# A Strassen-like feed-forward kernel: one of the seven products divided once more, over unit pairs and both passes

## The chip, the cores and the metric

The kernel runs on one core of a Trainium2 chip. The metric is the device time of one execution in microseconds, the median of several runs. The core's engines work side by side, each in its own program order: TensorE (PE, matmuls into eight PSUM banks of 128 x 512 f32), VectorE (DVE), ScalarE (ACT), GpSimd (POOL) and SyncE (SP, which issues the DMAs). They wait for each other through semaphores.

## What is computed

A gated feed-forward block on 2048 tokens, with Dm = 1024 and Df = 3584:

```python
def reference(x, w_gate, w_up, w_down):
    g = jnp.einsum("bsd,df->bsf", x, w_gate)
    u = jnp.einsum("bsd,df->bsf", x, w_up)
    h = _gelu(g) * u
    return jnp.einsum("bsf,fd->bsd", h, w_down)
```

All inputs are bf16, the output too.

## The kernel before

**Seven products for eight.** The gate and up products are done by the Strassen-Winograd scheme: two matrices cut into 2 x 2 blocks are multiplied with seven block products in place of eight, at the price of sums of blocks. The two raw products (of blocks as they are) run in bf16, the others in f32r, a full-rate form of f32, since sums of bf16 values don't fit bf16.

**Tiling.** The 2048 tokens go in two passes (`NPASS`) of 1024, two column halves of 512 each. The 3584 features go in 14 units (`NU`) of 256, two row halves of 128 each; the contraction over 1024 is halved too (`KH` = 4 blocks of 128 each). In a unit, every product is done for gate and up, with four matmuls of 512 columns each:

- two raw products (`raw_products`, L190), done for two units at once, at the end of every odd unit: 32 bf16 matmuls,
- p6 = s2·t2, p5 = s1·t1, p7 = s3·t3, p3 = s4·tb and p4 = A22·T4 (`unit`, L208): eight f32r matmuls each.

The t are sums of blocks of x, made by DVE once for each pass (`sums_t`; t4 is the last of a chain t1, t2, t4). The s are sums of blocks of the weights, eight POOL operations for each unit, one unit ahead (`make_s`, called in `prepare`, L658, right behind p5). `sa` is the block A22, cast to f32r by ACT.

**From banks to hT.** Products that belong together are added inside a bank where that is possible. Otherwise ACT copies a bank to SBUF (`snap`, L108; tiles p1, u2, p5), and DVE adds the copy to another bank (`add`; tiles sum). Then ACT makes the gelu of the gate half (`gelu`, L180), and DVE multiplies it with the up half into hT (`times`). Banks come in four pairs, which change their roles from unit to unit (L635). A product can begin only when the bank's last reader is done.

**Order.** The order on PE, DVE, POOL and SP is that of the program, by `manual_schedule`; ACT's too in the units. In pass 0, units 2 and up also make the sums of w_down that the second half of a pass needs (`keep_part`, L266): ACT copies a block into a bank that is free for a moment, DVE subtracts (tiles m, three for each unit). They stand behind p6 and ahead of p5's snaps and of `prepare`. They are kept in HBM (td). Small tiles in SBUF come from one ring of 52 slots (`slot`, L83): a new tile waits for the readers of the one that had the slot.

**Second half of a pass.** `down` (L464) multiplies hT with w_down, by a scheme of its own, and writes the output. In `more`, which it calls, x of the next pass is transposed by DMA and the sums t and s of the next pass's first unit are made.

**Helpers.** Every DVE sum goes through `dve` (L91), every POOL sum through `pool` (L94), every matmul through `matmul` (L112), so that the profile's rows are told apart by tiles.

Of the kernel before, what the change touches and what calls it, by code (L numbers as in the profile page):

```python
# [10 lines left out]
def kernel(  # L11
# [23 lines left out]
    nc = tc.nc  # L35
# [21 lines left out]
    NPASS = S // (2 * N)  # L57
    NU = NFB // 2
    NWARM = 7
    H, Q, R2 = NJ // 2, N // 2, range(2)  # L60
    SLOTS = 52
    LAG = 3
# [20 lines left out]
    def slot(shape, dtype, name):  # L83
        return kpool.tile(shape, dtype, name=name, tag="k")
# [5 lines left out]
    def dve(out, a, b, op):  # L90
        nc.vector.tensor_tensor(out=out, in0=a, in1=b, op=op)  # L91
# [9 lines left out]
    def cast(src, name, shape=None):  # L101
        t = slot(shape or [P, N], f32r, name)
        nc.scalar.copy(out=t, in_=src)  # L103
        return t

    def snap(ps, name):
        t = slot([P, N], f32, name)
        nc.scalar.copy(out=t, in_=ps)  # L108
        return t
# [40 lines left out]
    def sums_s(w, eng):  # L150
        GU = range(2)
        sh = [P, KH, P]
        a11, a21 = [[w[:, i, :KH, h : h + P] for i in GU] for h in (0, P)]
        a12, a22 = [[w[:, i, KH:, h : h + P] for i in GU] for h in (0, P)]
        return Sums(
            how={
                "s1": lambda q, GU=GU: [new(eng, a21[i], a22[i], ADD, "s1", sh) for i in GU],
                "s2": lambda q: [new(eng, q["s1"][i], a11[i], SUB, "s2", sh) for i in GU],
                "s3": lambda q: [new(eng, a11[i], a21[i], SUB, "s3", sh) for i in GU],
                "s4": lambda q: [new(eng, a12[i], q["s2"][i], SUB, "s4", sh) for i in GU],  # L160
                "sa": lambda q: [cast(a22[i], "sa", sh) for i in GU],
            }
        )

# [5 lines left out]
        t.make("t1", "t2", "t3", "tb", "t4")  # L170
        return t

    def make_s(w, eng):
        s = sums_s(w, eng)
        s.make("s1", "s2", "s3", "sa", "s4")
        return s

    def gelu(src):
        g = slot([P, N], f32, "g")
        nc.scalar.activation(g, src, ACT.Gelu_apprx_tanh)  # L180
        return g

    def times(fb, c, g, u):
        dve(hT[:, fb // NJ, fb % NJ, c, :], g, u, MUL)

    def product(ps, lhs, rhs, start):
        for k in range(KH):
            matmul(ps, lhs[:, k, :], rhs[k], start and k == 0, k == KH - 1)

    def raw_products(e, c, xT, w):  # L190
        for i in range(2):
            product(e[i], w[:, i, :KH, :P], [xT[0][:, k, :] for k in range(KH)], True)
        p1 = [snap(e[i], "p1") for i in range(2)]
        for i in range(2):
            b21 = [xT[0][:, KH + k, :] for k in range(KH)]
            product(c[i], w[:, i, KH:, :P], b21, True)
        return p1

    def add(ps, other):
# [4 lines left out]
    def finish_raw(u, c, p1):  # L204
        g, up = add(c, p1)
        times(2 * u, 0, gelu(g), up)

    def unit(u, banks, s, t, late, after_p5, aside, keep, ahead_of_p4, behind_p4):  # L208
        GU = range(2)
        e, c, d = banks  # L210
        aside(-2)
        g, up = late() if late else (None, None)
        aside(-1)
        for i in GU:
            product(e[i], s["s2"][i], t["t2"], False)
        aside(0)
        keep(0, c[0])
        u2 = [snap(e[i], "u2") for i in GU]
        if late:
            g = gelu(g)  # L220
        c11 = g, up
        keep(1, c[0])
        keep(2, c[1])
        c = d
        for i in GU:
            product(c[i], s["s1"][i], t["t1"], True)
        p5 = [snap(c[i], "p5") for i in GU]
        after_p5()
        for i in GU:
            product(e[i], s["s3"][i], t["t3"], False)  # L230
        g, up = new(dve, e[0], p5[0], ADD, "sum", dtype=f32), banks[1][not late]
        dve(up, e[1], p5[1], ADD)
        if late:
            times(2 * u, 0, *c11)
        for i in GU:
            product(c[i], s["s4"][i], t["tb"], False)
        times(2 * u + 1, 1, gelu(g), up)
        aside(1)
        g, up = add(c, u2)
        times(2 * u, 1, gelu(g), up)  # L240
        ahead_of_p4()
        for i in GU:
            product(e[i], s["sa"][i], t["t4"], False)
        behind_p4()
        times(2 * u + 1, 0, gelu(e[0]), e[1])

    td = dpool.tile([P, NJ, 3, N], f32, name="td")  # L250
    wraw, made = {}, {}

    def fetch_wd(js):
        big = None
        for j in js:
            if j < NJ - 2:
                wraw[j] = [slot([P, Dm], bf16, "raw") for _ in range(2)]
            else:
                if big is None:
                    big = wpool.tile([P, 4, Dm], bf16, name="w")  # L260
                n = 2 * (j - NJ + 2)
                wraw[j] = [big[:, n + kh] for kh in range(2)]
            for kh in range(2):
                nc.sync.dma_start(out=wraw[j][kh], in_=wdn[:, kh, j, :])
# [367 lines left out]
            return []  # L632
        return list(range(u - 2, NJ if u == NU - 1 else u - 1))

    E, K, C, F = odd, cc, dd, even  # L635

    def loaded(u):
        if u not in ws:
            ws[u] = load_w(u)
        return ws[u]  # L640

    def raw_of(u, e):
        p1 = raw_products(e, K, xT, loaded(u))
        return lambda: finish_raw(u, K, p1)

    for ip in range(NPASS):
        with tc.manual_schedule(engines={ENG.Activation}):
            if ip == 0:
                ws = {1: w, 2: ahead}
                late = lambda: add(cc, nxt["p1"])  # L650
            else:
                raw_of(0, F)()
                raw_of(1, C)()
            for u in range(1 if ip == 0 else 0, NU):
                js = making(u) if ip == 0 else []
                first = (ip, u) == (0, 1)

                def prepare():  # L658
                    if first:
                        pool_behind(t["t4"][-1])  # L660
                    if u + 1 < NU:
                        nxt["s"] = make_s(loaded(u + 1), pool)
                    if len(js) == 1:
                        store_made(js[0])
                    for j in js[1:]:
                        keep_whole(j)
                    if ip == 0:
                        fetch_wd(making(u + 1))

                def keep(part, ps):  # L670
                    if js:
                        keep_part(js[0], part, ps)

                def aside(part):
                    if first and part < 0:
                        rest_of_0(part + 2)
                    if part == 0 and u + 2 < NU:
                        loaded(u + 2)
                    if part == 0 and "t4" not in t:
                        t.make("t4")  # L680

                def ahead_of_p4():
                    if u % 2 and u + 1 < NU:
                        raw_of(u + 1, F)()
                        nxt["c11"] = raw_of(u + 2, C)

                def behind_p4():
                    if "c11" in nxt:
                        nxt.pop("c11")()

                if u % 2 and not first:
                    E, K, C = C, E, K
                banks = (E, K, C) if u % 2 else (F, K, E)
                unit(
                    u, banks, s, t, late if first else None, prepare, aside, keep,
                    ahead_of_p4, behind_p4,
                )
                s = nxt.pop("s", None)

        last = ip == NPASS - 1  # L700
        got, nxt = {}, {}

        def more(step):
            if last:
                return
            if step in (-1, 0, 2):
                store_made({-1: NJ - 3, 0: NJ - 2, 2: NJ - 1}[step])
            if step == 0:
                xT[:] = new_x()
            if step >= 24 and step % 2 == 0 and step // 2 - 12 < len(moves):  # L710
                c, ko = moves[step // 2 - 12]
                transposing(xT, c, ko, (2 * (ip + 1) + c) * N)
            if step == 50:
                ws.clear()
                ws.update({n: load_w(n) for n in range(2)})
            if step == 58:
                got["s"] = make_s(ws[0], dve)
            if step == 62:
                got["t"] = make_t(xT)

        down(ip, F + K, C + E, last, more)
        E, K, C, F = K, E, F, C
        if not last:
            t, s = got["t"], got["s"]

# [28 lines left out]
```

## Time and profile before

| | |
|---|---|
| median of 3 runs | 539.14 us (538.97 to 539.33) |
| the profiled execution | 539.29 us |
| its span | 537.5 us |
| mean granted clock of TensorE | 0.999 |
| PE busy | 532.7 us (99%), 2451 matmuls |
| DVE busy | 356.3 us (66%) |
| ACT busy | 258.1 us (48%) |
| POOL busy | 259.3 us (48%) |
| DMA | 93.30 MB, mean 174 GB/s |

The profile is of one execution. The span runs from the first to the last recorded instruction; 1.8 us lie outside of it. Of each engine it gives busy time and share of the span. The chain that ended last is followed back from the last instruction to what released it. In the rows of operations, "out<-in" names the tiles, then the shapes; xN is the number of instructions in the row, and where a row of the timeline ends in brackets, the engine was idle that long before it, and the name behind the arrow is what ended the idle time.

Two facts of order that are used below: unit 2 begins at 40.65 us, unit 3 at 49.72, unit 4 at 65.73, unit 5 at 74.80; the raw products of units 4 and 5 run from 56.98 to 63.71.

### The profile page before, as it was taken

The numbers are of one execution on the slowest core, as the hardware profiler recorded it, in microseconds if no ns is written. First come the engines' busy times: TensorE is split into PE (matmuls) and PEld (weight loads), VectorE is DVE, ScalarE is ACT, GpSimd is POOL, SyncE is SP. The second block draws the span as 40 slices with busy tenths as digits, with TensorE's granted clock in tenths as the row PEclk, the third lists the DMA queues.
The fourth block names the chain that finished last, engine by engine and source line by source line (L and its number), as shares of the span: only waits on it lengthen the run. The fifth ranks groups of instructions, "written<-read, shape, count | busy, mean of one in ns | idle before, by whom it ended". The sixth has DMA issues, their size and how long they took to land.

```text
span 537.5 us, 7573 instructions
## 1 busy us (share of the span) xinstructions
PE 532.7 (99%) x2451; PEld 382.4 (71%) x2451; DVE 356.3 (66%) x536; ACT 258.1 (48%) x457; POOL 259.3 (48%) x243
## 2 busy tenths in 40 slices
PE   8999999999999999999999999999999999999997
PEld 4568686867777746888868677776868685478887
DVE  2986766767676894595855464555554639979844
ACT  2556675666666410265355555555555551113340
POOL 1179966677773500000087767676766600000194
PEclk9999999999999999999999999999999999999999
DMA  9675666759482999999873233242520049573752
GB/s 245 156 186 168 186 177 176 218 136 262 131 234 71 383 357 298 308 197 275 264 187 88 78 80 81 77 119 50 145 57 23 2 130 390 204 236 88 243 169 70
DMA packets 108199, 93.30 MB, mean 174 GB/s; under 512 B 17280, under 2 KB 93056, under 8 KB 108160
## 3 DMA queue, kind: packets, MB, share of 16 engines
q1 hardware_dynamic: 108160, 92.82, 59.6%
q8 instruction: 20, 0.33, 0.3%
q14 instruction: 19, 0.16, 0.1%
HBM read 74.45 MB, written 15.20 MB: 167 GB/s over the span
## 4 chain that ended last, share of the span: by engine, by line
PE 98%; DMA 1%; SPq 0%; DVE 0%; issue 0%
PE bank L112 98%; DMA xn<-in_x_dram 1%; SPq L538 0%; DVE st L91 0%; PE bank L545 0%
## 5 line engine op out<-in xcount | busy, mean ns | idle before, releaser
L94 POOL TENSOR_TENSOR s<-w 128x512 fp32r<-128x512 bf16 x102 | 119.0, 1188 | 163.0 <-PE bank L112 113.5
L112 PE MATMUL bank<-t,s 128*128 128x512 f32 x648 | 151.7, 390 | 0.0
L112 PEld LDWEIGHTS bank<-t,s 128*128 128x128 f32 x648 | 121.7, 188 | 25.4
L112 PE MATMUL bank<-xT,w 128*128 128x512 bf16 (+1 forms) x504 | 109.7, 376 | 0.0
L108 ACT COPY p<-bank 128x512 f32<-128x512 f32 x124 | 69.8, 590 | 45.2 <-PE bank L112 45.1
L91 DVE TENSOR_TENSOR sum<-bank,p 128x512 f32<-128x512 f32 x54 | 37.3, 691 | 79.4 <-PE bank L112 78.3
L112 PEld LDWEIGHTS <-w 128*128 128x128 bf16 x504 | 48.1, 98 | 58.1 <-issue 3.4
L91 DVE TENSOR_TENSOR hT<-g,bank 128x512 bf16<-128x512 f32 x112 | 76.8, 688 | 17.6 <-PE bank L112 4.5
L180 ACT ACTIVATE g<-sum 128x512 f32<-128x512 f32 x81 | 51.4, 635 | 74.5 <-DVE sum L91 74.2
L94 POOL TENSOR_TENSOR q<-q 128x256 fp32r<-128x256 f32 x28 | 21.1, 788 | 80.0 <-PE bank L112 79.4
L112 PE MATMUL bank<-q 128*128 128x512 f32 x240 | 59.0, 389 | 0.0
L94 POOL TENSOR_TENSOR s<-w,s 128x512 fp32r<-128x512 bf16 x50 | 57.7, 1175 | 0.0
L94 POOL TENSOR_TENSOR s<-s,w 128x512 fp32r<-128x512 f32 x50 | 57.2, 1166 | 0.0
L112 PE MATMUL bank<-t,sa 128*128 128x512 f32 x216 | 55.9, 401 | 0.0
L112 PE MATMUL bank<-tb,s 128*128 128x512 f32 x216 | 53.3, 389 | 0.0
L108 ACT COPY u<-bank 128x512 f32<-128x512 f32 x62 | 35.5, 589 | 34.3 <-PE bank L112 34.2
L112 PEld LDWEIGHTS bank<-q 128*128 128x128 f32 x240 | 45.1, 188 | 9.3
L112 PE MATMUL bank<-raw,hT 128*128 128x512 bf16 x224 | 48.7, 379 | 0.0
L112 PEld LDWEIGHTS bank<-t,sa 128*128 128x128 f32 x216 | 40.6, 188 | 9.4
L103 ACT CAST tb<-raw 128x512 fp32r<-128x512 bf16 x28 | 17.2, 624 | 62.6 <-DMA raw<-in_w_down_dram 34.1
L112 PEld LDWEIGHTS bank<-tb,s 128*128 128x128 f32 x216 | 40.6, 188 | 8.4
L91 DVE TENSOR_TENSOR bank<-bank,p 128x512 f32<-128x512 f32 x54 | 37.7, 699 | 8.8 <-PE bank L112 6.2
(60 smaller groups left out, 493.8 us busy)
## 6 DMA issues: line engine op xcount, KB each, us to landing
raw<-in_w_down_dram SPq DMA_DIRECT2D x76, 256.0 KB, 5.1
q<-td SPq DMA_DIRECT2D x60, 256.0 KB, 4.9
w<-in_w_gate_dram SPq DMA_DIRECT2D x27, 512.0 KB, 5.9
w<-in_w_up_dram SPq DMA_DIRECT2D x27, 512.0 KB, 7.0
td<-m SPq DMA_DIRECT2D x12, 768.0 KB, 4.6
w<-td SPq DMA_DIRECT2D x6, 1024.0 KB, 10.1
out_dram<-st SPq DMA_DIRECT2D x32, 128.0 KB, 1.7
td<-w SPq DMA_DIRECT2D x2, 768.0 KB, 6.3
```

What stands on the lines that cost most here:

```text
L91: nc.vector.tensor_tensor(out=out, in0=a, in1=b, op=op)
L94: nc.gpsimd.tensor_tensor(out=out, in0=a, in1=b, op=op)
L103: nc.scalar.copy(out=t, in_=src)
L108: nc.scalar.copy(out=t, in_=ps)
L112: nc.tensor.matmul(ps, lhsT=lhs, rhs=rhs, start=start, stop=stop, skip_group_check=True)
L180: nc.scalar.activation(g, src, ACT.Gelu_apprx_tanh)
```

## The change

For the units 4 to 11, the product p4 is divided once more. Two neighbouring units a and b (4/5, 6/7, 8/9, 10/11: `SPLIT`) give two row blocks, the two passes give two column blocks, the contraction of four k blocks is halved: a 2 x 2 x 2 product of its own, for which seven half products are done in place of eight. A half product has four matmuls (two k blocks, gate and up).

- **Pass 0** does five of the seven at the end of unit b (`split_first`): A11·B11, A12·B21, s2·i2, sh·i4, s3·i3. That is 20 matmuls where p4 of the two units had 16. Two sums (z2, z3) that the other pass needs are copied by ACT and stored in HBM (dz).
- **Pass 1** does the other two in unit b, between p5 and p7 (`split_second`): s1·i1 and s4·t4[2:], 8 matmuls for 16. The stored sums are loaded during unit a, and DVE adds the product to all four.
- **Sums of weights** for a pair (`split_sums`): three more POOL operations for each pair and pass, behind `make_s` of unit b. In pass 1 the cast `sa` of these units goes; in pass 0 that of unit b becomes a half one (`sh`).
- **Sums over the passes.** The columns of B come from t4 of both passes, so t4 of pass 1 is made in pass 0. x of pass 1 is transposed by 16 DMAs in units 1 to 3 (`next_x`), into the part of hT that is still unused. In `prepare` of units 2, 3 and 4, DVE makes t4 of pass 1 from it (`next_t4`, three operations for each of four k blocks: 3, 6, 3). In `prepare` of units 4 and 5, DVE makes the inner sums i1 to i4 (`inner_i`, four operations each). i1 is stored in HBM (di) and loaded in pass 1 (`load_i1`).
- **Banks.** The four pairs get other names and another rotation. In pass 0 the raw products behind a divided pair run in another order: the first raw product of both units, then the second of each. Some hT products read other banks than before.

The core of the diff:

```diff
+    SPLIT = (4, 6, 8, 10)
+    NEXT_X = {1: (0,), 2: (1, 2), 3: (3,)}
+    NEXT_T4 = {2: ((0,), ()), 3: ((1, 2), ()), 4: ((3,), (0,)), 5: ((), (1,))}
...
+    def split_sums(wa, wb, ip):
+        ka, kb = slice(KH, KH + 2), slice(KH + 2, NKB)
+        a11, a12, a21, a22 = [w[:, :, k, P:] for w in (wa, wb) for k in (ka, kb)]
+        sh = [P, 2, 2, P]
+        q = {"s1": new(pool, a21, a22, ADD, "s1", sh)}
+        q["s2"] = new(pool, q["s1"], a11, SUB, "s2", sh)
+        if ip == 0:
+            q["s3"] = new(pool, a11, a21, SUB, "s3", sh)
+        else:
+            q["s4"] = new(pool, a12, q["s2"], SUB, "s4", sh)
+        return q
...
-    def unit(u, banks, s, t, late, after_p5, aside, keep, ahead_of_p4, behind_p4):
+    def unit(u, banks, s, t, late, after_p5, aside, keep, mid, behind_p7, p4):
...
         after_p5()
+        mid()
         for i in GU:
             product(e[i], s["s3"][i], t["t3"], False)
         g, up = new(dve, e[0], p5[0], ADD, "sum", dtype=f32), banks[1][not late]
         dve(up, e[1], p5[1], ADD)
+        more = behind_p7()
...
+    def split_first(a, ea, eb, z, s, sp, t):
+        sa = s["a"]["sa"]
+        half(z, lambda i, k: sa[i][:, k], t["t4"][:2], True)
+        z1 = [snap(z[i], "z1") for i in range(2)]
+        half(ea, lambda i, k: sa[i][:, 2 + k], t["t4"][2:], False)
+        g, up = plus(ea, z1)
+        half(z, lambda i, k: sp["s2"][:, i, k], t["i2"], False)
+        z2 = [snap(z[i], "z2") for i in range(2)]
+        gl = gelu(g)
+        times(2 * a + 1, 0, gl, up)
+        half(eb, lambda i, k: s["b"]["sh"][:, i, k], t["i4"], False)
+        half(z, lambda i, k: sp["s3"][:, i, k], t["i3"], False)
+        z3 = [snap(z[i], "z3") for i in range(2)]
+        g, up = plus(eb, z3)
+        for n, zs in enumerate((z2, z3)):
+            for i in range(2):
+                nc.sync.dma_start(out=dz[:, a // 2, n, i], in_=zs[i])
+        times(2 * a + 3, 0, gelu(g), up)
...
+    def split_second(a, ea, y, sp, t, z):
+        half(y, lambda i, k: sp["s1"][:, i, k], t["i1"], True)
+        half(ea, lambda i, k: sp["s4"][:, i, k], t["t4"][2:], False)
+        for n in range(2):
+            for i in range(2):
+                dve(z[n][i], y[i], z[n][i], ADD)
+        g, up = plus(ea, z[0])
+        times(2 * a + 1, 0, gelu(g), up)
...
+    def next_t4(k):
+        lo, hi = [[hT[:, 1, 6 + kk, c, :] for c in range(2)] for kk in (k, KH + k)]
+        q = new(dve, lo[1], lo[0], SUB, "t1")
+        q = new(dve, hi[1], q, SUB, "t2")
+        later[k] = new(dve, hi[0], q, SUB, "t4")
+
+    def inner_i(t, k):
...
+        b11, b21 = t["t4"][k], t["t4"][2 + k]
+        b12, b22 = later[k], later[2 + k]
+        i1 = new(dve, b12, b11, SUB, "i1")
+        dve(t["i2"][k], b22, i1, SUB)
+        nc.sync.dma_start(out=di[:, k], in_=i1.bitcast(f32))
+        dve(t["i3"][k], b22, b12, SUB)
+        t["i4"].append(new(dve, b21, t["i2"][k], SUB, "i4"))
...
                     if ip == 0:
                         fetch_wd(making(u + 1))
+                        if u in NEXT_T4:
+                            for k in NEXT_T4[u][0]:
+                                next_t4(k)
+                            for k in NEXT_T4[u][1]:
+                                inner_i(t, k)
```

## The prediction

> **What bounds the kernel now.** I read the page first: busy times, then the chain that ended last.
>
> ```profile
> span 537.5 us, 7573 instructions
> PE 532.7 (99%) x2451; PEld 382.4 (71%) x2451; DVE 356.3 (66%) x536; ACT 258.1 (48%) x457; POOL 259.3 (48%) x243
> ...
> PE 98%; DMA 1%; SPq 0%; DVE 0%; issue 0%
> ```
>
> TensorE (PE) carries 98% of the chain. The view of PE's waits holds only two, 0.8 and 0.6 us, both at the start. So a matmul taken out is worth its whole time, and any wait that the change brings to PE is added whole: there is no idle time on PE to take it up. The question is whether the other engines still finish ahead of PE. Next, the timeline of PE in units 5 and 6:
>
> ```profile
> 74.80 5.60 PE L112 MATMUL bank<-t,s 128*128 128x512 f32 x24
> 80.24 1.97 PE L112 MATMUL bank<-tb,s 128*128 128x512 f32 x8
> 82.06 7.08 PE L112 MATMUL bank<-xT,w 128*128 128x512 bf16 x32
> ```
>
> From start to start, 24 f32r matmuls take 5.44 us, 0.2267 each, and 32 bf16 ones 6.73. Then the windows view, with one row for each pair of units (25.1 us of PE work), says how much room the helpers have:
>
> ```profile
> 40.65:65.70 25.05, 25.05 (x113) 18.08 (x112) 17.35 (x26) 16.13 (x31) 25.05 (x24) 1.00 0.65 190
> 65.70:90.80 25.10, 25.10 (x113) 18.08 (x112) 17.45 (x26) 16.29 (x31) 18.57 (x17) 1.00 0.66 189
> 300.00:325.00 25.00, 25.00 (x114) 18.01 (x112) 13.41 (x21) 13.85 (x25) 18.01 (x17) 1.00 0.32 85
> ```
>
> The columns are PE, PEld, DVE, ACT, POOL. VectorE (DVE) has 7.7 us free in a pair of pass 0 and 11.6 in one of pass 1; GpSimd (POOL) has none in units 2 and 3, some 6.5 us later. Last, the timeline of DVE in unit 3, where the change puts most:
>
> ```profile
> 53.61 1.49 DVE L91 TENSOR_TENSOR m<-bank,m 128x512 fp32r<-128x512 f32 x2 [0.80 <-ACT bank L272]
> 55.01 0.68 DVE L91 TENSOR_TENSOR sum<-bank,p 128x512 f32<-128x512 f32 x1
> 55.61 0.69 DVE L91 TENSOR_TENSOR bank<-bank,p 128x512 f32<-128x512 f32 x1
> 56.70 0.69 DVE L91 TENSOR_TENSOR hT<-g,bank 128x512 bf16<-128x512 f32 x1 [0.40 <-ACT g L180]
> ```
>
> A DVE operation lasts 0.69 us; one that doesn't need the result just before it starts 0.60 us after it, one that does 0.80 (m, two in 1.49). The queue is in program order. In that order prepare stands behind the m's and ahead of the sum that takes p7 out of its bank, so what the change adds in prepare delays that sum.
>
> **What the change removes: matmuls.** The order of instructions of the two programs shows 2451 PE matmuls before and 2435 after. For each of the four pairs, pass 0 does 20 half-product matmuls in place of 16, pass 1 does 8 in place of 16: +16 and -32 in all. 16 x 0.2267 = **-3.6 us**. These sit in pairs 4 to 11, whose f32r matmuls have one rate.
>
> **What it adds beside PE.** DVE gets 68 operations: 20 in pass 0's units 2 to 5 (3, 6, 7, 4: next_t4 and inner_i), 16 in pass 0's pairs, 32 in pass 1's. POOL gets 24 (split_sums, 3 for each pair and pass, 1.13 each). ACT gets four. SP gets 16 transposes and 35 plain DMAs. I go by place.
>
> - Transposes of the next x, units 1 to 3: issued on SP, which idles between loads there; before's transposes take 1.1 to 1.3 us each to issue and land after 4.3. They land some microseconds before next_t4 reads them. 0; behind them on SP stand the raw loads of unit 3 (the one ending ACT's wait at 51.49), which at worst come 2 us late. I take 0.
> - Units 2 and 3, DVE alone. Unit 2: the m's end at 45.32; three dependent operations (2.2 us) put the p7 sum at 47.6, its end at 48.1 (PE lag included) where p4 would start at 47.91: +0.3. Unit 3: six operations (4.4 us) end at 59.5; then come the sum, the bank sum, the gelu on ACT and the hT product, which ends at 61.5. That product reads the bank that the next raw product of unit 4 writes, which PE reaches at 59.8: +1.8. Two further banks of the raws, handed on by DVE the same way, +0.37 each. Together **+2.8**.
> - Units 4 and 5, DVE alone: seven operations (4.9 us) and four (2.9), in a pair that has 7.7 us free in all and also takes 4 extra sums. Same order of reasoning, bank by bank: p5 of unit 5 waits for unit 4's hT product +1.6; p7 of unit 5 for the snaps of u2, which on ACT stand behind two late gelus, +1.4; p3 +0.3; the first half product of split_first for the hT product of unit 5, +3.0; the snap of z +0.5. **+6.8**. As a check: 15 x 0.7 = 10.5 us of added DVE work against 7.7 of room leaves 2.8 even if nothing was in the wrong order, and order costs the rest, as the m's come late in a unit (their ACT copies need the bank that PE frees).
> - Pairs 6 to 11 in pass 0: the snap of z1 (0.59) ahead of the half product that reuses z, about 0.15 each: **+0.45**.
> - Pass 1: DVE has 13.4 us in a pair, gains 8 x 0.69 and p4's banks need more hops: about 19 to 21 of 23.3 (25.1 less eight matmuls). The hT product ahead of the second raw bank is late by 0.15 to 0.4: **+1.6** for four pairs. POOL goes to 19 operations, 21.5 of 23.3 us: still covered, with 1.8 us to spare.
> - Stores and loads of z and i1 (256 KB, 4.6 to 5 us from issue to landing here) are issued half a unit or more ahead: 0; uncovered, 5 us once.
>
> **DVE against POOL.** The 20 operations in units 2 to 5 read two tiles in SBUF; nearly all of before's DVE operations there read a PSUM bank instead, and are not slowed by POOL (0.69 all through 30 to 66 us with POOL busy). Where two-SBUF operations met POOL, the timeline shows:
>
> ```profile
> 270.04 2.50 DVE L91 TENSOR_TENSOR t<-xT,t 128x512 fp32r<-128x512 bf16 x4
> 270.35 4.30 POOL L94 TENSOR_TENSOR s<-w 128x512 fp32r<-128x512 bf16 x2 [86.06 <-PE bank L112]
> ...
> 507.50 1.22 DVE L91 TENSOR_TENSOR q<-hT,q 128x512 fp32r<-128x512 bf16 x1
> 508.65 1.22 DVE L91 TENSOR_TENSOR q<-hT 128x512 fp32r<-128x512 bf16 x1
> ```
>
> At 270 DVE kept going and POOL's two operations took 4.30 us for the usual 2.27; at 507, where POOL ran two of half the size, DVE took 1.22 for 0.69. So one waits for the other, and both outcomes exist. next_t4 is a chain (t1, t2, t4), which leaves DVE empty for 0.1 us between operations, so I expect POOL to get in. A first operation then waits half a POOL operation (0.55), each dependent one up to 1.13 + 0.6 - 0.8 = 0.95 more. Unit 2, POOL back to back: 0.55 + 2 x 0.95 = 2.4. Unit 3, where POOL has about two operations of s(4) left: 1.5. Unit 4: 1.5; unit 5: 0.6. **+6.0**; bounds 0 (as at 270) and +12 (every one of the 20 meets POOL, and PE pays two thirds).
>
> The Trainium skill (SBUF — State Buffer, "Who interferes with whom") says that such a DVE operation and a GpSimd operation that reads SBUF block each other fully, and that the one that starts first goes first; by that rule alone, POOL being busy, the sum would take the +6.0. The rows at 507 agree, the row at 270 only if the four count as one.
>
> **Sum.** 539.3 (the profiled execution; its span is 537.5, the median of the runs 539.14) - 3.6 + 2.8 + 6.8 + 6.0 + 0.45 + 1.6 = **553.4 us**.
>
> **Rivals.**
> - *DVE keeps the memory to itself* (as at 270): term 6.0 falls to about 1. 548.4. For it: same shapes as at 270. Against: the chain's gaps.
> - *Faster: the bursts are covered.* DVE and ACT work off the delay before PE comes to the bank, because PE's next products need other banks first. Then only unit 2's 0.3, 0.45 and about 1 in pass 1 are left: 537.4. For it: 7.7 us free per pair, and POOL and DMA nowhere late. It decides if unit 3's hT product ends before 59.8, that is if its six operations take under 2.7 us in place of 4.4; for that they would have to start before the m's end. Against: program order.
> - *Every operation meets POOL*: +12 in place of +6.0, 559.4, with PE pauses of several microseconds. The page's row of granted clock is full speed throughout, with no pause over 0.8 us. The Trainium skill (TensorE: Matmul & The Clock Gate, Part 1) puts the return to half speed after an idle window of about 3.4 us; nothing in this trace tests it, and by it each such pause would cost about 1.7 us more.
> - *POOL is late in pass 1*: at a mean of 1.30 us per operation (DVE's two-SBUF sums beside it) 19 take 24.7 of 23.3 us: +1.4 a pair, 5.6 in all: 557.4 (553.4 - 1.6 + 5.6).
> - *It doesn't do what it says*: the count of matmuls excludes this.
>
> **Chances.** Forecast (550 to 557) 0.42; DVE keeps (544 to 550) 0.27; every operation meets POOL 0.10; POOL late in pass 1 0.06; covered 0.12; within 0.2% of before (about what a measurement of this kernel can tell from no change), the two sides cancelling, 0.03. Slower 0.85, faster 0.12. The range leaves out the covered and equal cases and the worst of the upper: 542 to 561; the forecast alone has 550 to 557.
>
> **What would show it.** Right: PE waits of 10 us or more in all between 45 and 100 us, released by DVE hT products and sums; PE busy 3.6 us lower; added DVE operations at over 1 us where POOL works; next to nothing in pairs 6 to 11 of pass 0. Wrong: PE without waits at 60 and at 85 us (covered), added operations at 0.69 (DVE keeps), or PE waiting in pass 1 for s tiles (POOL late).

## The result, and the profile after

The changed kernel takes 563.13 us (median of 4 runs, 562.28 to 564.38) against 539.24 for the one before: a ratio of 1.0446, with a 95% interval of 1.0422 to 1.0469. That is 23.9 us slower, where 14.2 were forecast; it lies 2.1 us above the range. The profiled execution took 564.38, its span is 562.5.

The page of the changed kernel, the same three lines as before:

```profile
span 562.5 us, 7718 instructions
PE 538.2 (96%) x2414; PEld 380.5 (68%) x2435; DVE 403.2 (72%) x604; ACT 258.1 (46%) x461; POOL 290.5 (52%) x267
...
PE 74%; DVE 7%; DMA 7%; ACT 6%; issue 3%; POOL 1%; SPq 1%; DVEq 0%; ACTq 0%; POOLq 0%
```

PE fell from 98% of the chain to 74%. Its busy time rose by 5.5 us although 16 matmuls are gone (the weight loads, x2435, show them all; 21 matmul records are missing). What PE waits for, with total, number and longest:

```profile
PE bank L115 <- DVE hT L94: 7.7, 7, 4.7
PE bank L115 <- DVE sum L94: 5.4, 1, 5.4
PE bank L115 <- ACT u L111: 1.8, 4, 0.8
PE bank L115 <- DMA raw<-in_w_down_dram: 1.7, 2, 1.4
```

Where the time went is read from the start of p6 of each unit, in the timelines of PE before and after. Differences, against what the prediction's terms give for the same stretch:

| stretch | measured | forecast |
|---|---|---|
| units 2 and 3, and the raws behind them | +9.6 | +6.7 (2.8 + 2.4 + 1.5) |
| units 4 and 5 | +10.55 | +9.8 (0.9 for four more matmuls, 6.8, 2.1) |
| units 6 to 11 of pass 0 | +8.6 | +3.2 (2.7 matmuls, 0.45) |
| units 12 and 13, w_down | +2.3 | 0 |
| units 4 to 11 of pass 1 | -6.4 | -5.7 (-7.25 matmuls, +1.6) |
| the rest | +0.2 | 0 |

**The largest pause** is one operation. Timelines of DVE, POOL and PE in unit 2 of the changed kernel:

```profile
45.23 6.12 DVE L94 TENSOR_TENSOR t<-hT 128x512 fp32r<-128x512 bf16 x1
51.38 1.42 DVE L94 TENSOR_TENSOR t<-hT,t 128x512 fp32r<-128x512 bf16 x2
...
46.30 2.28 POOL L97 TENSOR_TENSOR s<-w,s 128x512 fp32r<-128x512 bf16 x2
48.55 2.24 POOL L97 TENSOR_TENSOR s<-w 128x512 fp32r<-128x512 bf16 x2
52.22 2.72 POOL L97 TENSOR_TENSOR s<-s,w 128x512 fp32r<-128x512 f32 x2 [1.43 <-DVE t L94]
...
53.45 3.78 PE L115 MATMUL bank<-t,sa 128*128 128x512 f32 x8 [5.39 <-DVE sum L94]
```

The first operation of next_t4 lasts 6.12 us in place of 0.69. POOL runs on without a gap until 50.79; there its next sum needs the slot that DVE's t holds, it stops, and 0.6 us later DVE's operation is done. The 5.39 us of PE follow.

The second pause comes from unit 4, where DVE's operations took turns with POOL's. Four of the seven lasted 1.37 to 1.65 us, and unit 4's hT product, for which p5 of unit 5 waits, came late (DVE, then PE):

```profile
79.84 0.71 DVE L94 TENSOR_TENSOR t<-hT 128x512 fp32r<-128x512 bf16 x1
80.75 2.94 DVE L94 TENSOR_TENSOR t<-hT,t 128x512 fp32r<-128x512 bf16 x2 [0.20 <-DVE t L94]
83.61 1.65 DVE L94 TENSOR_TENSOR i<-t,t 128x512 fp32r<-128x512 f32 x1
...
90.15 2.08 PE L115 MATMUL bank<-t,s 128*128 128x512 f32 x4 [4.70 <-DVE hT L94]
```

**The clock.** The windows view, for the matmuls behind the two longest pauses (the last three columns are the granted clock, the DMA share, GB/s):

```profile
53.45:57.03 3.58, 3.58 (x8) 2.81 (x9) 3.13 (x5) 2.12 (x4) 3.58 (x4) 0.50 1.09 158
90.15:95.80 5.65, 5.38 (x12) 3.81 (x13) 4.65 (x8) 4.99 (x10) 4.50 (x5) 0.52 0.14 32
```

Eight matmuls took 3.58 us, where they take 1.81 at full clock. Added over both places, PE lost some 5 us in this way (1.8 and 0.5 behind the first pause, 1.2 and 1.5 behind the second). The prediction had this only inside a rival. The Trainium skill (TensorE: Matmul & The Clock Gate, Part 1) puts the return to half speed behind an idle window of about 3.4 us, and the return to full speed behind about 3.4 us of sustained work. Half speed behind pauses of 5.4 and 4.7 us agrees with the first; behind the second pause it lasted longer than 3.4 us (0.52 over 5.65 us).

**The pairs.** In units 6 and 7 of the changed kernel, from the timelines of SP, ACT and PE (the two rows at the end are ACT's for the same load in the kernel before):

```profile
115.95 0.34 SPq L393 DMA_DIRECT2D td<-m  x1
116.40 1.33 SPq L374 DMA_DIRECT2D raw<-in_w_down_dram  x2
...
121.80 0.59 ACT L382 CAST bank<-raw 128x512 f32<-128x512 bf16 x1 [2.18 <-DMA raw<-in_w_down_dram]
122.33 1.07 ACT L111 COPY u<-bank 128x512 f32<-128x512 f32 x2
...
123.05 2.06 PE L115 MATMUL bank<-t,s 128*128 128x512 f32 x8 [0.85 <-ACT u L111]
...
101.69 0.59 ACT L272 CAST bank<-raw 128x512 f32<-128x512 bf16 x1 [1.85 <-DMA raw<-in_w_down_dram]
102.21 1.07 ACT L108 COPY u<-bank 128x512 f32<-128x512 f32 x2
```

The load of unit 7's w_down rows is issued behind the store of unit 6's m's. It lands at 121.8. ACT's cast waits for it, the snaps of u2 stand behind the cast, and p7 waits for the snaps. Before, the cast waited for the same load too, but the snaps ended at 103.28, some 0.2 us before p7 (by the matmuls of unit 7, which began at 99.88, p7 began at about 103.5). Now unit 6 has lost its p4 to the end of unit 7, and unit 7 begins 7.47 us after unit 6 in place of 9.07.

### The profile page after: what moved, and what is told of

The parts are those of the page before. It is cut to its first block, busy times and chain, and to the rows that moved or that the text cites. A ratio compares the mean times of both kernels' runs of the same rounds, so it can differ in the third digit from the quotient of the medians.

```text
span 562.5 us, 7718 instructions
## 1 busy us (share of the span) xinstructions
PE 538.2 (96%) x2414; PEld 380.5 (68%) x2435; DVE 403.2 (72%) x604; ACT 258.1 (46%) x461; POOL 290.5 (52%) x267
## 4 chain that ended last, share of the span: by engine, by line
PE 74%; DVE 7%; DMA 7%; ACT 6%; issue 3%; POOL 1%; SPq 1%; DVEq 0%; ACTq 0%; POOLq 0%
PE bank L115 74%; DMA raw<-in_w_down_dram 5%; DVE t L94 2%; ACT bank L382 1%; ACT g L196 1%; DVE sum L94 1%; POOL w L97 1%; DMA w<-in_w_down_dram 1%; DVE hT L94 1%; ACT p L111 1%; DMA xn<-in_x_dram 1%; ACT u L111 1%; DVE m L94 1%; ACT sa L106 1%; DVE i L94 1%
## 5 line engine op out<-in xcount | busy, mean ns | idle before, releaser
L97 POOL TENSOR_TENSOR s<-w 128x512 fp32r<-128x512 bf16 x114 | 135.8, 1211 | 157.0 <-PE bank L115 100.6
L115 PE MATMUL bank<-t,s 128*128 128x512 f32 x664 | 162.0, 398 | 6.5 <-DVE hT L94 4.7
L115 PEld LDWEIGHTS bank<-t,s 128*128 128x128 f32 x664 | 126.4, 191 | 36.2 <-DVE hT L94 5.1
L196 ACT ACTIVATE g<-sum 128x512 f32<-128x512 f32 x97 | 61.4, 633 | 118.2 <-DVE sum L94 116.1
L111 ACT COPY p<-bank 128x512 f32<-128x512 f32 x124 | 68.6, 589 | 39.0 <-PE bank L115 38.5
L97 POOL TENSOR_TENSOR s<-s,w 128x512 fp32r<-128x512 f32 x58 | 67.5, 1184 | 3.4 <-DVE t L94 1.4
L97 POOL TENSOR_TENSOR s<-w,s 128x512 fp32r<-128x512 bf16 x54 | 62.5, 1180 | 0.3
L94 DVE TENSOR_TENSOR q<-hT 128x512 fp32r<-128x512 bf16 x56 | 39.7, 709 | 5.6 <-PE bank L115 5.6
L115 PEld LDWEIGHTS <-hT 128*128 128x128 bf16 x224 | 21.7, 98 | 28.6 <-issue 2.8
```

The source lines that it names most:

```text
L97: nc.gpsimd.tensor_tensor(out=out, in0=a, in1=b, op=op)
L115: nc.tensor.matmul(ps, lhsT=lhs, rhs=rhs, start=start, stop=stop, skip_group_check=True)
```

## Experiments

Theories: **A**, DVE's operations with two operands in SBUF are held by POOL (and how); **B**, the two take turns; **C**, the transposes that write beside what DVE reads hold it; **D**, transfers tuned to the old length of a unit come late. Rivals: the added operations cost by their place in the queue alone; the divided pairs have too many steps. All times are medians; the kernel before ran beside each (539.2 to 539.6).

### DVE against POOL

**One operation alone, in the kernel before** (`probe` is a tile that nobody reads):

```diff
 def prepare():
+    if (ip, u) == (0, 2):
+        dve(probe, xT[0][:, 0], xT[1][:, 0], SUB)
```

> The kernel before, with one DVE operation added in unit 2, behind the m's (at about 45.2 us): a difference of two x tiles in SBUF into a tile that nobody reads. Theory A (whichever of DVE and POOL runs back to back keeps the shared memory access until it has a gap of its own): POOL runs without a gap until it needs a slot that the sum behind the added operation frees, 21 operations of 1.13 us after 30.65, at about 54.3; so the operation lasts about 9 us in place of 0.69, p4 of unit 2 waits about 7 us, and with slower matmuls behind the pause the time is 546 to 549. Theory B (they take turns): at most 1.8 us, the time 539.2 to 539.8. Theory C (the 6.1 us of the changed kernel's first added operation come from the DMA transposes that write beside what it reads): none are here, 539.2.

Two executions: 538.79, the profiled one, in which the operation got in at once, and 548.40, which has no trace. The second time is the one that theory A gives; what was held in it is not shown.

```profile
44.73 0.76 DVE L91 TENSOR_TENSOR probe<-xT,xT 128x512 bf16<-128x512 bf16 x1
```

**The same with a PSUM operand:**

```diff
-        dve(probe, xT[0][:, 0], xT[1][:, 0], SUB)
+        dve(probe, banks[1][1], xT[1][:, 0], SUB)
```

> The same added operation, but its first operand is a PSUM bank. Theories A and B: no meeting with POOL, 0.69 us, the time 539.2 to 539.5. If the place in DVE's queue were what costs: the same as with two SBUF operands.

539.43, ratio 0.9998 (0.9987 to 1.0009); the operation took 0.68. Its place in the queue costs nothing.

**Both behind each other**, so that the one with two SBUF operands comes 0.6 us later:

```diff
+        dve(probe, banks[1][1], xT[1][:, 0], SUB)
         dve(probe, xT[0][:, 0], xT[1][:, 0], SUB)
```

> The kernel before with two added DVE operations in unit 2: one with a PSUM operand, and behind it the one with two SBUF operands, which so comes 0.6 us later against POOL's operations than in the run where it stood alone (there one execution took 538.8 and the other 548.4). Theory A1 (what decides is whether the operation comes while POOL hands over from one operation to the next): the outcome changes from execution to execution again, 539 or 548. Theory B (turn by turn): never above 540.5.

548.82, ratio 1.0170 (1.0153 to 1.0187), 548.25 to 549.64 in all four executions. Theory A's length came out, its changing outcome (A1) didn't. DVE, then POOL, then PE, in that run:

```profile
45.42 0.68 DVE L91 TENSOR_TENSOR probe<-bank,xT 128x512 bf16<-128x512 f32 x1
46.13 8.45 DVE L91 TENSOR_TENSOR probe<-xT,xT 128x512 bf16<-128x512 bf16 x1
54.51 0.68 DVE L91 TENSOR_TENSOR sum<-bank,p 128x512 f32<-128x512 f32 x1
...
53.15 1.15 POOL L94 TENSOR_TENSOR s<-w 128x512 fp32r<-128x512 bf16 x1
55.26 1.16 POOL L94 TENSOR_TENSOR s<-w 128x512 fp32r<-128x512 bf16 x1 [0.96 <-DVE sum L91]
...
55.24 3.78 PE L112 MATMUL bank<-t,sa 128*128 128x512 f32 x8 [6.98 <-DVE sum L91]
```

The operation ends 0.3 us after POOL's run does, at the POOL sum that was named beforehand: the one whose slot the sum behind the operation frees. No transpose runs there, so theory C isn't needed for such a hold. The Trainium skill (SBUF — State Buffer, "Who interferes with whom") says that issue order decides who blocks, and of DVE's two-port modes that whoever issues first has the shared ports for its whole instruction; here POOL kept DVE's operation out over seven instructions.

**POOL's sums in an order with gaps**, all else as in the last run:

```diff
-        s.make("s1", "s2", "s3", "sa", "s4")
+        for i in range(2):
+            s[f"one{i}"] = how["s1"](s, (i,))[0]
+            s[f"two{i}"] = new(eng, s[f"one{i}"], w[:, i, :KH, :P], SUB, "s2", [P, KH, P])
+            s[f"four{i}"] = new(eng, a12[:, i], s[f"two{i}"], SUB, "s4", [P, KH, P])
...
+        s.make("s3", "sa")
```

> The kernel before with the two added DVE operations of the run that always came out at 548.8, and POOL's sums in another order: s1, s2 and s4 of the gate half, each needing the one just before it, then those of the up half, then s3. POOL's operations then start 1.25 us apart in place of 1.13, as its dependent ones do. Theory A2 (POOL keeps DVE out only while its operations follow without a gap; a dependent one leaves a gap): the second added operation takes at most 2 us, and the time is 539 to 540. Rival A3 (POOL keeps the access over such short gaps too): 7 us or more for the operation, 547 or more.

539.29, ratio 0.9998 (0.9988 to 1.0007). The operation took 0.43, between two POOL sums that now start 1.24 us apart:

```profile
45.86 0.43 DVE L91 TENSOR_TENSOR probe<-xT,xT 128x512 bf16<-128x512 bf16 x1
...
44.77 1.17 POOL L94 TENSOR_TENSOR s<-s,w 128x512 fp32r<-128x512 f32 x1
46.01 1.31 POOL L94 TENSOR_TENSOR s<-w,s 128x512 fp32r<-128x512 bf16 x1
```

**The changed kernel, its 20 operations with a PSUM operand each** (`ps` is the bank that the m's have just left; the operations of `inner_i` likewise):

```diff
-        q = new(dve, lo[1], lo[0], SUB, "t1")
-        q = new(dve, hi[1], q, SUB, "t2")
-        later[k] = new(dve, hi[0], q, SUB, "t4")
+        q = new(dve, ps, lo[0], SUB, "t1")
+        q = new(dve, ps, q, SUB, "t2")
+        later[k] = new(dve, ps, q, SUB, "t4")
```

> The changed kernel, with one operand of each of the 20 added DVE operations of units 2 to 5 replaced by a PSUM bank (the sums over the passes are then not those of the reference). Theory A: the first lasts 0.69 in place of 6.12, PE's pause in unit 2 falls from 5.4 to about 0.3 us, that in unit 4 from 4.7 to about 1.6, no half-rate stretch is left behind them: 549 to 553. Rival (the queue of 20 operations alone is what costs): 561 to 563. The transposes (theory C): the first operation still reads what a DMA transposed, and stays at 6 us.

553.49, ratio 1.0261 (1.0192 to 1.0330): 9.6 us less than the change, and half a microsecond above the expected range. The two executions lie 3 us apart (552.00 and 554.97). The first operation:

```profile
44.58 0.68 DVE L94 TENSOR_TENSOR t<-bank,hT 128x512 fp32r<-128x512 f32 x1
45.29 1.42 DVE L94 TENSOR_TENSOR t<-bank,t 128x512 fp32r<-128x512 f32 x2
```

The first operation still reads what a transpose wrote, so the transposes (theory C) didn't hold it. In the profiled execution (552.00) the granted clock is 1.0 throughout, and the longest pause is 2.4 us: with the long pauses the half-rate stretches are gone too. The other execution has a mean clock of 0.991 and no trace.

**POOL stopped around the operations** (in `make_s`, behind the first sums, POOL waits for the last of them; loads as in the first run of the next group):

```diff
+        s.make(*names[:n])
+        pool_behind(burst())
+        s.make(*names[n:])
```

> The changed kernel with the loads ahead of the store, and with POOL made to stop around each of the four groups of added operations: behind the first sums of s (two kinds in units 2 and 3, three in 4 and 5) it waits for the group's last result. Theory A: DVE's operations last 0.69 again, PE's pauses are those of the queue alone: 547 to 551. Rival (POOL's stops make its s tiles late, and PE waits for those): 555 or more.

553.93, ratio 1.0265 (1.0250 to 1.0280): 4.7 less than with the loads alone, but over the forecast. In units 2 and 4 it works (all operations at 0.7); in unit 3 the first operation takes 1.1; in unit 5 POOL is late from its stops and still in its run, and three of the four operations take 1.5 to 1.6:

```profile
86.39 0.85 DVE L94 TENSOR_TENSOR i<-t,t 128x512 fp32r<-128x512 f32 x1
87.27 1.53 DVE L94 TENSOR_TENSOR xT<-t,i 128x512 fp32r<-128x512 f32 x1
88.73 1.63 DVE L94 TENSOR_TENSOR xT<-t,t 128x512 fp32r<-128x512 f32 x1
...
94.02 2.92 PE L115 MATMUL bank<-t,sa 128*128 128x512 f32 x6 [5.36 <-DVE hT L94]
```

**The order with gaps, in the changed kernel** (the order as above; loads at the unit's start, as in the second run of the next group):

```diff
-                        nxt["s"] = make_s(loaded(u + 1), pool, casts)
+                        nxt["s"] = make_s(loaded(u + 1), pool, casts, ip == 0 and u < 6)
```

> The changed kernel with the loads at the unit's start (557.3), and POOL's sums of s made in units 1 to 5 in the order with gaps (s1, s2, s4 of the gate half, then of the up half, then s3). Theory A2: no added operation takes over 2.3 us; the pause in unit 2 falls from 3 to 5 us to under 1.5, the total to 551 to 554. Rival A3 (a chain of DVE operations is caught anyway): 556 or more.

558.51, ratio 1.0358 (1.0333 to 1.0382), against 557.29 with the loads alone: no gain. No operation is held for a whole run any more (the longest takes 1.65), but many take turns:

```profile
44.86 1.44 DVE L94 TENSOR_TENSOR t<-hT 128x512 fp32r<-128x512 bf16 x1
46.34 3.10 DVE L94 TENSOR_TENSOR t<-hT,t 128x512 fp32r<-128x512 bf16 x2
```

Three operations take 4.6 us; the pause in unit 2 is 2.3 (3.2 without the gaps, where the first operation was held for 3.99 in that run), and unit 3's grows from 1.0 to 2.2, since POOL is later there. The part of A2 on being caught held, its time didn't.

### The late loads

**The load ahead of the store** (in `prepare`):

```diff
+                    if ip == 0:
+                        fetch_wd(making(u + 1))
                     if len(js) == 1:
                         store_made(js[0])
...
-                    if ip == 0:
-                        fetch_wd(making(u + 1))
```

> The changed kernel, with the loads of the next w_down rows issued ahead of the store of m in place of behind it. Theory D (in pairs 6 to 11 of pass 0, unit a is shorter by p4's eight matmuls, 1.8 us, so that the raw load issued behind its m's lands too late for ACT's cast in unit b, and the snaps of u2 behind it keep p7 waiting): a pair goes from 27.7 to 26.1 us, the time to about 558. Rival (ACT and DVE have too many steps in unit b): unchanged, 563.

558.65, ratio 1.0357 (1.0325 to 1.0388): -4.5. Units 6 to 11 go from 28.3, 27.8 and 27.8 us a pair to 27.2, 26.2 and 27.1, and down loses its 2 us.

**The load at the unit's start** (in `aside`, ahead of the m's; the store stays):

```diff
+                    if part == 0 and ip == 0:
+                        fetch_wd(making(u + 1))
                     if part == 0 and u + 2 < NU:
                         loaded(u + 2)
```

> The changed kernel with nothing else altered than the loads of the next w_down rows issued at the unit's start. Theory D: pairs 6 to 11 at 26.0 to 26.3 us each in place of 27.8, and down's late loads gone: 557 to 558.7. Rival (DVE's operations of units 2 to 5 are all that matters): 562 to 564.

557.29, ratio 1.0331 (1.0311 to 1.0351): -5.8, though the pairs are at 27.3, 26.3 and 27.7.

**Without the 20 operations, loads as in the change:**

```diff
-    NEXT_T4 = {2: ((0,), ()), 3: ((1, 2), ()), 4: ((3,), (0,)), 5: ((), (1,))}
+    NEXT_T4 = {}
```

In the matmuls t4 stands where the missing sums would; the stores and the load of i1 go with them.

> The changed kernel with the 20 DVE operations left out (t4 in the place of the sums over the passes) and nothing else altered; the raw loads stand behind the store of m as in the change. Theory A+D: the pauses of units 2 to 5 go, the 1.7 us a pair and 2 us in down stay: 541.5 to 544. Rival (the late loads were themselves a consequence of the pauses in units 2 to 5): 538 or less.

546.70, ratio 1.0142 (1.0121 to 1.0162), more than either side expected. Without the long pauses of units 2 to 5, the pairs 6 to 11 still take 28.6, 28.4 and 27.6.

**Without them, load ahead of the store; and load at the unit's start** (the last edit, with each of the two edits of the loads):

> The changed kernel with the loads issued ahead of the store of m, and without the 20 added DVE operations of units 2 to 5: the sums over the passes are left out, t4 itself stands in their place (the output is then not the reference's); all matmuls, POOL operations, transposes, stores and loads stay otherwise. Theory A (DVE's 20 operations are the whole loss of units 2 to 5): no pause of PE in units 2 to 5, and the -3.6 us of matmuls come out less the small waits of pass 1 and the pairs: 536.0 to 538.0. Rival (banks, ACT chain and POOL sums of the divided pairs cost as much by themselves): 541 or more.

> As the run without the 20 added operations (the sums over the passes left out, t4 in their place), but the loads of the next w_down rows are issued at the unit's start, ahead of its m's, and the store of m stays where it was: neither waits for the other. Theory D (the raw load behind m's store delays p7 in unit b; with the load ahead of the store it was the store that came late, and the next unit's m's waited for their only tile): both waits go, and a pair costs 26.0 us: 535.8 to 537.3. Rival (the divided pairs have other waits of that size): 538.5 or more.

540.40, ratio 1.0018 (1.0007 to 1.0030), and 541.45, ratio 1.0039 (1.0023 to 1.0055). Both missed their ranges (up to 538 and 537.3). The chain of the second shows what is late next:

```profile
96.70 0.70 DVE m L94
97.42 5.17 DMA td<-m
102.58 0.03 issue
102.61 0.05 DVEq L94
102.66 0.04 issue
102.70 0.70 DVE m L94
```

There is one tile for the m's. Unit 7's first m waits until unit 6's are stored, 5.2 us; ACT's next casts and p5's snaps stand behind it.

**Two m tiles**, on top of the last run (the ring of slots makes room):

```diff
-    SLOTS = 52
+    SLOTS = 49
...
-    mpool = ctx.enter_context(tc.tile_pool(name="m", bufs=1))
+    mpool = ctx.enter_context(tc.tile_pool(name="m", bufs=2))
```

> Without the 20 operations, the loads at the unit's start, and two m tiles in place of one (three slots fewer in the ring of small tiles, 49 for 52), so that the m's of unit b don't wait for the store of unit a's. Theory D2 (with the load no longer late it is this store that keeps p7 and the chain behind it waiting, 0.8 us a pair): pairs at 26.0 to 26.2 us, 536.3 to 538. Rival (POOL's s tiles or ACT's chain are as late): 539 or more.

537.42, ratio 0.9970 (0.9961 to 0.9979): 1.8 us less than before, as forecast. Pairs 6 to 11 at 26.5, 26.1 and 26.1, against 25.08 + 0.91 = 25.99 for the matmuls alone. Windows view, one pair:

```profile
118.31:144.44 26.13, 26.08 (x118) 18.71 (x117) 19.78 (x31) 18.64 (x35) 21.52 (x20) 1.00 0.71 221
```

The pair at the same place without the 20 operations and with the loads as in the change:

```profile
122.28:150.71 28.43, 26.98 (x117) 18.47 (x117) 19.68 (x31) 18.76 (x35) 21.40 (x20) 1.00 0.66 204
```

DVE, ACT and POOL do the same work in both. The stretch is 2.3 us longer in the second; 1.4 of it is PE idle, the rest lies in matmuls that the profile draws longer. Only the place of the loads, the second tile and the three slots given up for it differ.

**PSUM operands and the load at the unit's start together** (the two edits above):

> The changed kernel with PSUM operands in the 20 added operations (so none meets POOL; the sums over the passes are not the reference's) and the loads issued at the unit's start. Theory A+D: the two losses add up, 553.5 less 4.5: 547 to 550. What is left above the run without the 20 operations is the cost of their place in DVE's queue: 10 to 13 us.

550.61, ratio 1.0204 (1.0179 to 1.0230), just above the expected 547 to 550. The savings (9.6 and 5.8) add up only to 12.5.

### Versions that were to beat both

**Two pairs divided, the operations spread** over units 4 to 9, in even units between the first and second m, loads ahead of the store; then the same with the gaps, two m tiles and loads at the unit's start:

```diff
-    SPLIT = (4, 6, 8, 10)
-    NEXT_X = {1: (0,), 2: (1, 2), 3: (3,)}
+    SPLIT = (8, 10)
+    NEXT_X = {1: (0,), 2: (2,), 3: (1,), 4: (3,)}
...
+    SPREAD = {4: 4, 5: 3, 6: 4, 7: 3, 8: 4, 9: 2}
```

> The loads ahead of the store, only the pairs 8/9 and 10/11 divided, and the 20 operations spread over the units 4 to 9: 4 in each even unit between the first and the second m, where DVE and POOL both idle, 2 or 3 in each odd unit in prepare. Theory A: the gain of two pairs is 1.8 us, the spread operations find DVE idle and POOL between two runs: 537.8 to 540. Rival (any operation that meets POOL is caught for microseconds, and DVE has no room): 543 or more.

> Only pairs 8/9 and 10/11 divided, the 20 operations spread over units 4 to 9, loads at the unit's start, two m tiles (49 slots), POOL's sums in units 3 to 8 in the order with gaps. Theories A2 and D2: what was lost in units 6 to 9 of the spread version (9 of its 10 us) falls to a third: 539 to 543. For it to beat the kernel before, all of it would have to go: 537.5. Rival: as without these, 547 to 549.

549.25, ratio 1.0176 (1.0160 to 1.0191), and 553.95, ratio 1.0270 (1.0252 to 1.0287). In units 4 and 5 of the first, where POOL rests between two runs, the operations cost PE 0.4 us in all; from unit 6 on POOL's runs lie elsewhere, most operations of units 6 and 8 take 1.4 to 1.7, and units 6 to 9 lose 9.7 us beyond their four more matmuls. The gaps make POOL's runs longer and the meetings more.

**The 20 operations on POOL**, two and three pairs divided, two m tiles and loads at the unit's start (the second: `SPLIT = (6, 8, 10)`, `SPREAD = {2: 4, 3: 5, 4: 5, 6: 6}`):

```diff
-    SPREAD = {4: 4, 5: 3, 6: 4, 7: 3, 8: 4, 9: 2}
+    SPREAD = {4: 4, 5: 4, 6: 4, 7: 4, 8: 4}
...
-        q = new(dve, lo[1], lo[0], SUB, "t1")
+        q = new(pool, lo[1], lo[0], SUB, "t1")
```

> Pairs 8/9 and 10/11 divided, the 20 operations done by POOL, four in each of the units 4 to 8, behind the s sums; loads at the unit's start and two m tiles (49 slots). POOL has 12 operations, 13.6 us, in a unit of 12.5 and is some 8 us ahead, so it stays ahead. Theory A+D2: two pairs are worth 1.8 us, nothing waits: 537.3 to 538.2, faster than before and the changed kernel. Rival (POOL falls behind, PE waits for s): 540 or more.

> The same with pairs 6/7, 8/9 and 10/11 divided, and POOL's 20 operations in units 2 (4), 3 (5), 4 (5) and 6 (6). POOL runs without a gap from 30 us to unit 7 and is there just in time at best: three pairs are worth 2.7 us, 536.6 to 537.5 if it is; rival: PE waits for s tiles or inner sums in units 5 to 7, 538 to 545.

546.56, ratio 1.0132 (1.0118 to 1.0146), and 553.16, ratio 1.0248 (1.0234 to 1.0262). POOL wasn't late with s tiles: the ring of slots was. By the profile's releasers, DVE's sum behind the raws waits for one of POOL's operations, which frees a slot (DVE, then PE, of the first run):

```profile
116.48 0.69 DVE L94 TENSOR_TENSOR sum<-bank,p 128x512 f32<-128x512 f32 x1 [5.66 <-POOL xT L97]
...
117.22 3.57 PE L115 MATMUL bank<-xT,w 128*128 128x512 bf16 x8 [2.98 <-DVE sum L94]
```

No kernel that does the whole computation beat the one before.

## Why the prediction was wrong

The direction was right, and that DVE's added operations in units 2 to 5 would carry it. The sum was 11.0 us short of the profiled execution: by the table, 7.7 in units 6 to 13 and w_down and 3.6 in units 2 to 5, less 0.8 in pass 1; 0.5 is spread over the rest. Either of the first two alone would have left the result inside the range. Of the signs named, the pauses released by DVE between 45 and 100 us came (12.5 us); PE's busy time didn't fall by 3.6, and pairs 6 to 11 didn't stay at next to nothing.

- **Matmuls, -3.6.** Right: 2435 weight loads for 2451, and in the run without the 20 operations and with the transfers in place almost half of it is left over (537.42 against 539.2).
- **Pairs 6 to 11 of pass 0, +0.45, and "stores and loads ... 0".** This is the larger step that failed. Measured: +5.9 in the pairs (8.6 less 2.7 of matmuls) and +2.3 in units 12, 13 and w_down. I had costed the new transfers and the new snaps, and not the old transfers against the new length of unit a. Moving p4 out of it takes 1.6 us from a chain (m's, store, load, cast, snap, p7) that before had ended just in time. The runs without the 20 operations show it alone: 546.70 with the transfers as they are, 537.42 with early loads and two m tiles. The 9.3 us between them are a little more than the 8.2 measured in place. Their timelines show why: pair 4/5 has the same chain and takes 27.85 us in the first and 25.89 in the second, which in the changed kernel lies under the pauses.
- **DVE against POOL, 6.0, "bounds 0 and +12".** The second step that failed is "a first operation then waits half a POOL operation (0.55)": it waited 5.4 us, until POOL's run ended. Of the two readings that the rows of before allowed, one going on and one taking turns, the row at 270 had the answer, with the roles changed: whoever runs without a gap can keep the other out for the whole run. I had used it only in DVE's favour. Unit 3's six operations, priced at 1.5, met nothing (0.68 to 0.69 each): POOL idled there from 59.4 to 69.86. The profile puts that wait down to a weight load, but the load landed at 69.95, after POOL had begun; a gelu on ACT that ended at 69.84 fits, as the release of a slot. In cost the term is 563.13 - 553.49 = 9.6, some 5 of it by the clock behind the pauses; with the loads at the unit's start it is 557.29 - 550.61 = 6.7.
- **The queue, 2.8 + 6.8 = 9.6.** By medians, the 20 operations with PSUM operands cost 553.49 - 546.70 = 6.8, and with the loads at the unit's start 550.61 - 541.45 = 9.2. So the two terms can't be told apart to better than some 3 us: where PE already waits for a late load, a late DVE probably costs less. Together they are 16.4 and 15.8, where 15.6 were forecast. That agreement is luck as far as POOL's part goes: unit 4's operations took turns much as forecast, though at twice the price (3.3 for 1.5), but the largest part was one long hold and the half clock, which the sum doesn't have.
- **Pass 1, +1.6.** Measured +0.8: the hT products were late in one pair only. The rival of a late POOL didn't come.
- **The rivals.** "Every operation meets POOL", 559.4, came nearest in time, by another mechanism. The covered case, 537.4, was wrong in that the operations could be covered; a run came to its time (537.42), but only without the operations and with the old transfers moved.

Open: why the single operation got in at once in one execution and was held 8.45 us in the shifted run. In the first it came 0.68 us after POOL's operation had begun, in the second 0.81, in the change 0.05; in unit 4 of the change, at 1.01, it got in (there POOL's next sum needs the one before, and began 1.25 us after it). A rule that fits all four wasn't found. Nor is it shown that the gaps alone let DVE in, since one_op got in once without them; that no operation of the run with gaps in the changed kernel lasted over 1.7 us speaks for it.

## What to carry to other kernels

A DVE operation with two SBUF operands, put beside a GpSimd engine that runs without a gap, can cost what is left of that run and not one operation (8.45 and 6.12 us here, though 0.76 in one execution); a PSUM operand took it out of the matter (0.68). When a change makes a stage shorter, list the transfers that are issued in it and used in the next one, and their slack: a store and a load that were in time by less than what the stage lost become the bound. And long pauses of PE are paid a second time: in the profiled executions of these runs matmuls at half clock followed every pause of 2.9 us and more, and some shorter ones (a pause of 2.04 us in the spread version, but not one of 2.50 in the same run).

## What the runs showed of the hardware that was not expected

POOL kept DVE's two-SBUF operation waiting over seven of its operations (8.45 us, against 0.43 for the same operation where nothing held it), and let it through with 1.24 us between the starts of its operations in place of 1.13. Where both have such operations queued, they can also take turns, at 1.4 to 1.7 us for each DVE operation. Behind a pause of 5.4 us the granted clock was 0.50 for 3.6 us.
